# A hand-written order of attention and feed-forward steps, searched anew: which loads go first, and nine unread products inside one cluster

## The chip, the cores and the metric

One core of a Trainium2 chip runs the whole kernel. The core has five engines with queues of their own: TensorE (PE, matrix products into PSUM), VectorE (DVE), ScalarE (ACT), GpSimd (POOL) and SyncE (SP, which here only issues transfers). Each engine works through its queue in order and waits on semaphores. The metric is the time of one execution on the device in microseconds; lower is better.

## What is computed

Linear attention with a decay for each head, block by block, followed by a feed-forward layer with a leaky activation:

```python
for b in range(nb):                                   # blocks of 64
    intra = np.einsum('bhic,bhjc->bhij', qb, kb) * Dmask[None]
    intra = np.einsum('bhij,bhjd->bhid', intra, vb)
    inter = np.einsum('bhid,bhde->bhie', qb * lam_pow[None], kv_state)
    out[:, :, sl] = intra + inter
    kv_state = lam_block * kv_state + np.einsum('bhsd,bhse->bhde', kb * rev_pow, vb)
x = out.transpose(0, 2, 1, 3).reshape(B * S, H * D)
h = x @ w_in
g = np.maximum(h, 0.0) + alpha * np.minimum(h, 0.0)
y = g @ w_out
```

q, k and v are 4 x 8 x 768 x 64 (sequences, heads, positions, head width), w_in is 512 x 2048 and w_out 2048 x 512, all in fp32.

## The kernel before

The work is cut into six chunks of 512 tokens (`NC`), each of two sequences by 256 positions. A unit `n` is a chunk, one of its two sequences and one half of the heads, so units 0 to 3 are chunk 0, units 4 to 7 chunk 1, and so on up to 23.

For each unit `cast` writes q and k as halves (`qk16`), `turn` transposes them on PE and `turned` copies the result out of PSUM (later units are transposed by a load, `turn_by_dma`, on SP). `decayed` multiplies q by its decay (`qdT`) and `key_decayed` k by its own (`kdec`, four buffers). `decay_mask` and `causal` make the mask. `cluster(old, new)` is a run of small products on PE: for the older unit the state's part (L344) and the masked scores by v (L374), for the newer one the scores (L362) and then k by v (L391), which `state` and `spread` turn into the next state (`R`, `RD`). `masked` multiplies scores by the mask on DVE, and `out_of` copies the finished rows into `xT`.

The feed-forward part of a chunk `c` goes by sixteen blocks `f` of 128 columns: `up(c, f, bi, slot)` multiplies xT by w_in into a bank of PSUM (`bi` names one sequence, `None` both), `below` makes the lower branch on ACT, `gate` joins the branches on DVE (with `oma`, the slopes that `slopes` gets from alpha by a transposition on PE) and thereby frees the bank. `down` multiplies by w_out. From chunk 2 on the down product, and in chunk 5 also the up product, is done with seven products of sums of blocks in place of eight products (`product`, `up_block`, with `weight_sum`, `gate_sum`, `win_sum` and `x_sum`).

w_in is loaded in four pieces (`load_win(i)`, blocks 4i to 4i+3) and w_out likewise (`load_wout(i)`), all on POOL's queue and turned into halves on the way, as are v and the first q's (`load16`). k and the later q's are loaded in fp32 (`load`) on SP, or on POOL with `ring=1`. `hold` is a one-element memset on DVE ahead of a load, which keeps the load from being issued before DVE gets there. `fill(n, slot)` is `n` products of the identity with itself whose result nobody reads.

What runs when is written out by hand: a list of some 950 calls, one step a line, ends the kernel function. Each call appends its instructions to the queues of the engines that it names, so the list sets the order on every engine, and semaphores do the rest. PSUM has banks 0, 1 and 2 for `up` and `down`, `tk` for transposed tiles and the second half of products, two for scores and two for `acc`. A cluster called with `other=True` takes banks 0 and 1 in place of `acc`.

Of the kernel before, what the change touches and what calls it, by code (L numbers as in the profile page):

```python
# [11 lines left out]
def kernel(  # L12
# [315 lines left out]
    def cluster(old, new, other=False):  # L328
# [53 lines left out]
        if new is not None:  # L382
            t["kv"] = kv
            for hp in range(2):
# [62 lines left out]
    G = {}  # L447
# [343 lines left out]
    positions()  # L791
    load_alpha()
    identity()
    load("k", 0, 0, 0)
    distances()
    zeros(2, 1, "G")
    zeros(1, 1)
    logs()
    load16("q", 0, 0, 1)
    load("k", 0, 0, 1)  # L800
    fill(16, 2)
    key_decay(1)
    key_decay(0)
    load("q", 0, 0, 0)
    load16("v", 0, 0, 0)
    fill(36, 2)
    zeros(0, 1, "G")
    cast(0, "k", "V")
    hold("k", 1, 0)
    zeros(1, 0, "G")  # L810
    hold("k", 0, 1, 0)
    decay_mask(1, 1)
    key_decayed(1, "V")
    decay_mask(1, 0)
    cast(1, "k", "G")
    state_decay()
    decay_mask(0, 0)
    decay_mask(0, 1)
    cast(1, "q", "V")
    causal(0, 1)  # L820
    decay_mask(3, 0)
    cast(0, "q", "G")
    decay_mask(2, 0)
    load16("q", 0, 1)
    load("k", 0, 1, 1)
    turn(0)
    decay_mask(2, 1)
    query_decay(1)
    causal(1, 0)
    fill(5, 2)  # L830
    turned(0, "A")
    cast(3, "k", "A")
    zeros(0, 0)
    query_decay(0)
    key_decayed(0, "V")
    load16("v", 0, 0, 1)
    load16("v", 0, 1)
    load("k", 0, 1, 0)
    query_decay(3)
    fill(6, 2)  # L840
    turn(1)
    turned(1, "A")
    causal(0, 0)
    cluster(None, 0)
    fill(15, 2)
    key_decayed(3, "V")
    zeros(3, 1)
    key_decayed(2, "V")
    fill(17)
    spread(0, 1, "A", True)  # L850
    masked(0, 1)
    masked(0, 0)
    decay_mask(3, 1)
    load_win(0)
    cast(2, "k", "A")
    cast(2, "q", "V")
    cast(3, "q", "A")
    query_decay(2)
    state(0, 0)
    turn(2)  # L860
    causal(1, 1)
    load("k", 1, 0)
    decayed(0, "G")
    turned(2, "A")
    cast(5, "k", "V")
    slopes(2)
    load16("q", 1, 0)
    cluster(0, 1, True)
    state(0, 1)
    masked(1, 0)  # L870
    masked(1, 1)
    load16("v", 1, 0)
    decayed(1, "G")
    turn(3)
    spread(1, 1, "A", True)
    cluster(1, None)
    load_win(1)
    state(1, 0)
    hold("k", 3, 0)
    cast(4, "k", "A")  # L880
    out_of(0, "V")
    out_of(1, "A")
    load16("q", 1, 1)
    decayed(2, "V")
    state(1, 1)
    cluster(None, 2)
    masked(2, 1)
    hold("k", 2, 1)
    turned(3, "A")
    up(0, 0, 0, 2)  # L890
    spread(2, 1, "A", True)
    state(2, 0)
    load_win(2)
    masked(2, 0)
    key_decayed(4, "G")
    decayed(3, "G")
    below(0, 0, 0)
    gate(0, 0, 0)
    cast(4, "q", "G")
    cluster(2, 3, True)  # L900
    up(0, 2, 0, 2)
    load_win(3)
    spread(8, 0, "A")
    hold("k", 2, 0)
    cast(6, "q", "G")
    below(0, 2, 0)
    masked(3, 0)
    cast(7, "q", "G")
    spread(3, 1, "A", True)
    state(2, 1)  # L910
    state(3, 0)
    masked(3, 1)
    cast(5, "q", "V")
    state(3, 1)
    key_decayed(5, "G")
    zeros(2, 0, "G")
    turn(4)
    spread(11, 0, "V")
    out_of(2, "A")
    gate(0, 2, 0)  # L920
    cluster(3, None)
    fill(14, 0)
    load16("v", 1, 1)
    out_of(3, "A")
    turned(4, "V")
    load_wout(1)
    up(0, 1, 0, 0)
    below(0, 1, 0)
    up(0, 3, 0, 2)
    up(0, 6, None, 1)  # L930
    below(0, 3, 0)
    below(0, 6, None)
    gate(0, 1, 0)
    turn(5)
    cluster(None, 4)
    zeros(3, 0)
    state(4, 0)
    gate(0, 3, 0)
    gate(0, 6, None)
    turned(5, "A")  # L940
    decayed(5, "G")
    load_wout(0)
    hold("k", 1, 1)
    load("k", 1, 1)
    up(0, 2, 1, 0)
    below(0, 2, 1)
    decayed(4, "G")
    masked(4, 1)
    load_wout(2)
    up(0, 5, None, 2)  # L950
    up(0, 4, None, 1)
    state(4, 1)
    load("k", 2, 0, ring=1)
    gate(0, 2, 1)
    up(0, 0, 1, 0)
    below(0, 5, None)
    below(0, 4, None)
    gate(0, 5, None)
    below(0, 0, 1)
    up(0, 8, None, 2)  # L960
    gate(0, 0, 1)
    cast(6, "k", "G")
    below(0, 8, None)
    up(0, 3, 1, 0)
    spread(12, 0, "G")
    key_decayed(6, "G")
    gate(0, 4, None)
    gate(0, 8, None)
    below(0, 3, 1)
    up(0, 7, None, 1)  # L970
    masked(4, 0)
    spread(4, 1, "A")
    gate(0, 3, 1)
    load_wout(3)
    up(0, 1, 1, 2)
    cluster(4, 5)
    below(0, 7, None)
    cast(7, "k", "G")
    up(0, 9, None, 0)
    below(0, 1, 1)  # L980
    out_of(4, "A")
    state(5, 0)
    gate(0, 7, None)
    gate(0, 1, 1)
    up(0, 11, None, 2)
    below(0, 9, None)
    up(0, 14, None, 1)
    spread(5, 1, "A")
    below(0, 11, None)
    masked(5, 1)  # L990
    state(5, 1)
    gate(0, 9, None)
    below(0, 14, None)
    masked(5, 0)
    gate(0, 11, None)
    gate(0, 14, None)
    turn(6)
    key_decayed(7, "G")
    up(0, 12, None, 0)
    below(0, 12, None)  # L1000
    up(0, 10, None, 2)
    turned(6, "V")
    cluster(5, None)
# [767 lines left out]
```

## Time and profile before

| | |
|---|---|
| median of 3 runs | 209.84 us (209.22 to 210.29) |
| profiled execution, whole | 210.01 us |
| its span in the profile | 208.2 us |
| PE busy | 198.1 us |
| DVE busy | 173.2 us |
| ACT busy | 124.8 us |
| POOL busy | 124.5 us |
| bytes moved by transfers | 33.03 MB |
| unread products | 109, busy 9.8 us |

The profile is one execution. Its views are: a table of forty equal slices with the busy share of each engine in tenths, a list of who waited for whom, the chain of work that ended last, groups of like instructions with their mean time, the time from issue to landing of transfers, and a timeline in order of time. In a timeline row the first number is the start in microseconds from the start of the span, the second the length of the run of instructions, and `[2.72 <-POOL ident]` says how long the engine had been idle before it and what ended that. PE's matmuls overlap, so the sum of its busy time is no measure of how close it is to its peak; the distance between the starts of like products is.

### The profile page before, as it was taken

To read this page: it belongs to the slowest core of one execution; us is meant where nothing else is said; L and a number is where in the kernel's file an instruction comes from. 1 tells how busy PE (TensorE), PEld (TensorE's weight loads), DVE (VectorE), ACT (ScalarE), POOL (GpSimd) and SP (SyncE) were. 2 spreads that over 40 slices of the span, in tenths; PEclk is the share of its full clock that TensorE was granted. 3 is DMA by queue.
4 is the path that set the end of the run, shared out by engine and by line. 5 is a ranking of instruction groups with operands and counts; after the bars stand their busy time and mean duration, and the time that the engine had idled before them with its cause. 6 is when DMAs were issued, how large, how long until landed. Compare 5 with 4: busy or idle time off the path is not lost.

```text
span 208.2 us, 5964 instructions
## 1 busy us (share of the span) xinstructions
PE 198.1 (95%) x2382; PEld 134.7 (65%) x2382; DVE 173.2 (83%) x353; ACT 124.8 (60%) x257; POOL 124.5 (60%) x159
## 2 busy tenths in 40 slices
PE   4896899999999999999999999999999999999993
PEld 4874655565564564555556667776766688888882
DVE  3897889877587999788988899989978879998941
ACT  3997668753496644564777574646456567665320
POOL 8987289951293885787699542590389657235000
PEclk9999999999999999999999999999999999999999
DMA  4999999999999999999999899288160103102223
GB/s 114 272 188 191 200 216 167 199 285 204 137 302 244 240 278 202 291 261 157 202 230 172 108 194 186 74 213 97 23 131 2 55 0 105 50 0 78 76 76 126
DMA packets 61835, 33.03 MB, mean 159 GB/s; under 512 B 34528, under 2 KB 58608, under 8 KB 61808
## 3 DMA queue, kind: packets, MB, share of 16 engines
q0 software_dynamic: 22384, 13.24, 43.2%
q1 hardware_dynamic: 38096, 17.31, 37.5%
q10 hardware_dynamic: 1328, 2.11, 2.8%
q8 instruction: 18, 0.29, 0.6%
q14 instruction: 9, 0.07, 0.1%
HBM read 27.28 MB, written 6.29 MB: 161 GB/s over the span
## 4 chain that ended last, share of the span: by engine, by line
PE 76%; DMA 7%; issue 5%; POOL 4%; DVE 4%; ACT 1%; SPq 0%; POOLq 0%; DVEq 0%; ACTq 0%
PE h_ps L457 34%; PE p_ps L601 16%; PE o_ps L491 14%; DMA w_in_sb<-in_moe_w_in_dram 4%; PE s L362 3%; PE h_pb L705 3%; DMA qraw<-in_q_dram 3%; PE acc L374 2%; PE acc L344 2%; DVE g L752 2%; PE acc L391 1%; POOL win_sum L661 1%; POOL m L740 1%; DVE g L481 1%; POOL vh L102 1%
## 5 line engine op out<-in xcount | busy, mean ns | idle before, releaser
L457 PE MATMUL h_ps<-xT,w_in_sb 128*128 128x512 f16 (+1 forms) x352 | 77.3, 360 | 1.4 <-DMA w_in_sb<-in_moe_w_in_dram 0.9
L481 DVE SCALAR_TENSOR_TENSOR g<-m,oma,h_ps 128x512 f16<-128x512 f32 (+1 forms) x88 | 59.7, 694 | 15.7 <-ACT m L468 14.7
L468 ACT ACTIVATE m<-h_ps 128x512 f32<-128x512 f32 (+1 forms) x88 | 48.0, 558 | 34.3 <-PE h_ps L457 31.4
L457 PEld LDWEIGHTS <-w_in_sb 128*128 128x128 f16 x352 | 33.2, 98 | 30.9 <-issue 1.6
L601 PEld LDWEIGHTS <-g 128*128 128x128 f16 x320 | 31.1, 98 | 6.7 <-issue 0.2
L403 DVE TENSOR_TENSOR sm<-s,dmask 128x512 f16<-128x512 f32 x48 | 32.1, 683 | 1.4 <-PE s L362 1.4
L491 PE MATMUL o_ps<-w_out_sb,g 128*128 128x512 f16 x128 | 29.8, 379 | 0.0
L279 POOL TENSOR_TENSOR kdec<-kraw,kdecay 128x512 f16<-128x512 f32 x15 | 16.0, 1069 | 10.3 <-DMA kraw<-in_k_dram 6.9
L491 PEld LDWEIGHTS <-g 128*128 128x128 f16 x128 | 12.1, 98 | 13.5
L601 PE MATMUL p_ps<-wsum,g 128*128 128x256 f16 x160 | 20.6, 273 | 0.0
L601 PE MATMUL p_ps<-w_out_sb,g 128*128 128x256 f16 x160 | 19.9, 273 | 0.0
L252 POOL COPY RD<-R 64x128 f16<-64x128 f16 x30 | 9.1, 305 | 15.5 <-DVE R L428 14.6
L321 POOL TENSOR_TENSOR qdT<-qkT,qdecay 128x512 f16<-128x512 f16 (+1 forms) x15 | 15.9, 1064 | 3.1 <-DMA qkT<-qk 1.7
L248 ACT ACTIVATE xT<-acc 128x512 f16<-128x512 f32 x17 | 10.1, 596 | 8.0 <-PE acc L391 3.7
L625 ACT ACTIVATE o_sb<-p_ps 128x512 f32<-128x512 f32 (+1 forms) x20 | 10.2, 510 | 7.4 <-PE p_ps L601 7.1
L601 PEld LDWEIGHTS <-gsum 128*128 128x128 f16 x128 | 12.4, 98 | 2.7 <-DVE gsum L573 0.5
L428 DVE SCALAR_TENSOR_TENSOR R<-R,rdecay,acc 128x64 f16<-128x64 f16 x60 | 13.7, 273 | 0.6 <-ACT xT L248 0.3
L248 ACT ACTIVATE RD<-R 64x128 f16<-64x128 f16 x36 | 11.0, 306 | 2.8 <-DVE R L428 2.3
L238 PE MATMUL op_fill<-ident 128*128 128x128 f16 x109 | 9.8, 262 | 2.9 <-POOL ident masks.py:199 2.7
L601 PE MATMUL p_ps<-wsum,gsum 128*128 128x256 f16 x96 | 12.1, 273 | 0.2 <-DVE gsum L573 0.2
L581 POOL DMA_DIRECT2D g<-g x6 | 5.9, 978 | 10.7 <-PE p_ps L601 8.4
L102 POOL DMA_DIRECT2D vh<-in_v_dram x13 | 12.0, 926 | 0.0
(111 smaller groups left out, 315.4 us busy)
## 6 DMA issues: line engine op xcount, KB each, us to landing
out_dram<-o_sb SPq DMA_DIRECT2D x32, 128.0 KB, 2.0
kraw<-in_k_dram SPq DMA_DIRECT2D x7, 512.0 KB, 5.8
qraw<-in_q_dram SPq DMA_DIRECT2D x6, 512.0 KB, 6.9
vh<-in_v_dram POOLq DMA_DIRECT2D x11, 256.0 KB, 7.6
w_in_sb<-in_moe_w_in_dram POOLq DMA_DIRECT2D x4, 512.0 KB, 9.7
w_out_sb<-in_moe_w_out_dram POOLq DMA_DIRECT2D x4, 512.0 KB, 9.3
out_dram<-o_sb ACTq DMA_DIRECT2D x8, 256.0 KB, 5.5
kraw<-in_k_dram POOLq DMA_DIRECT2D x3, 512.0 KB, 10.2
```

Source lines behind the costliest of these rows:

```text
L102: nc.gpsimd.dma_start(out=rows16(x, c, bi)[:, ds(h0, n), :], in_=source({"q": q, "v": v}[x], c, bi, h0, n))
L248: nc.scalar.activation(out, in_, AF.Copy)
L279: engine(eng).tensor_tensor(out=kdec, in0=kr, in1=d.unsqueeze(3).to_broadcast([128, 2, 4, D]), op=ALU.mult)
L321: engine(eng).tensor_tensor(out=x, in0=y, in1=d.unsqueeze(2).to_broadcast([128, 4, n, 64]), op=ALU.mult)
L403: nc.vector.tensor_tensor(out=t["sm"][hl], in0=t["s"][hl], in1=mask_of(hl, units[n][2]), op=ALU.mult)
L428: nc.vector.scalar_tensor_tensor(out=then[:, hp], in0=R[b, hh, i][:, hp], scalar=rdecay[:, 2 * hh + hp : 2 * hh + hp + 1], in1=kv[:, hp], ...
L457: nc.tensor.matmul(h_ps[:, 0:n] if bi is None else h_ps[:, 0:n].rearrange("p (e j) -> p e j", e=2), lhsT=w_in_sb[:, gi, ts(f, 128)], rhs=x ...
L468: nc.scalar.activation(m[:, 0:n], HP[c, f, bi][:, 0:n], AF.Relu, scale=-1.0)
L481: nc.vector.scalar_tensor_tensor(out=g, in0=mv, scalar=oma[:, f : f + 1], in1=hv, op0=ALU.mult, op1=ALU.add)
L491: nc.tensor.matmul(O[c, t], lhsT=gated(c, f)[:, t // 2, t % 2, :], rhs=w_out_sb[:, f, :], start=(f == 0), stop=(f == NF - 1),)
L601: nc.tensor.matmul(acc, lhsT=lhsT, rhs=rhs, start=(first and j == 0), stop=(j == NJ - 1), skip_group_check=True,)
L625: nc.scalar.activation(o, acc, AF.Copy, scale=-1.0 if k in (7, 4) else 1.0)
```

## The change

`cluster` gets a parameter that puts unread products between its scores and its k by v, one call of it uses this, and the whole list of calls is replaced by another one. The steps are the same: the same products, the same loads, the same casts. What differs is their order and, for some hundred of them, the engine that does them.

```diff
-    def cluster(old, new, other=False):
+    def cluster(old, new, other=False, pad=0):
...
         if new is not None:
             t["kv"] = kv
+            if pad:
+                fill(pad, 2)
...
-    cluster(0, 1, True)
+    cluster(0, 1, True, 9)
...
-    load_win(1)
+    load("k", 1, 1, ring=1)
```

In the start, the new list has three memsets of `RD` on POOL ahead of the identity, 36 unread products, `slopes`, and 16 more ahead of `turn(0)` (before: 16, 36, `turn(0)`, and `slopes` behind `turn(2)`); the 32 products that stood behind `cluster(None, 0)` stand ahead of it, the 14 that stood behind `cluster(3, None)` stand ahead of `up(0, 0, 0)`. `load_win(1)` is ahead of `load16("v", 1, 0)` and `load_win(2)` ahead of `load16("q", 1, 1)`; `load_win(3)` is behind `key_decayed(5)`. `load_wout` goes in the order 0, 1, 2, 3 (before 1, 0, 2, 3), the last behind `weight_sum(1, 0, "G")`, which was on DVE. Four loads of k and q change between SP and POOL: `load("k", 1, 1)` goes to POOL, `load("k", 2, 1)`, `load("k", 3, 0)` and `load("q", 3, 0)` to SP. On DVE there are fewer `key_decayed` (6 for 9) and `decayed` (5 for 9), and more `out_of` (four more) and `win_sum` (11 for 7).

More of the change, by code (lines that the diff above doesn't have):

```diff
@@ L972 @@
[L972 to L995, printed above, removed]
@@ L996 @@
-    gate(0, 14, None)
-    turn(6)
-    key_decayed(7, "G")
[L999 to L1003, printed above, removed]
+    decayed(1, "G")
+    masked(1, 0)
+    state(1, 0)
+    state(1, 1)
+    cluster(1, None)
+    turned(2, "A")
+    key_decayed(2, "G")
+    out_of(1, "A")
+    cast(4, "k", "A")
+    turn(3)
+    out_of(0, "V")
+    cluster(None, 2)
+    turned(3, "V")
+    fill(14, 0)
+    up(0, 0, 0, 2)
+    masked(2, 0)
+    spread(2, 1, "A", True)
@@ L1115 @@
[L1115 to L1136 removed]
+    down(0, 3, 1, 2)
@@ L1247 @@
[L1247 to L1257 removed]
+    cluster(12, 13)
+    masked(13, 1)
+    cast(17, "q", "G")
+    up(2, 3, None, 0)
+    gate(2, 1, None)
+    weight_less(0)
+    below(2, 3, None)
+    out_of(12, "V")
+    down(1, 3, 0, 2)
+    gate(2, 3, None)
+    load("q", 4, 1)
+    weight_sum(3, 1, "G")
@@ L1565 @@
+    gate_sum(4, 4, 0, "k")
     up(4, 14, None, 0)
```

1416 lines of the change are left out of this document (709 added, 707 removed).

## The prediction

> **What bounds the kernel now.** I read the page's table of slices first, then the chain of waits, the waits of PE, and the timeline of the first 45 us.
>
> ```profile
> span 208.2 us, 5964 instructions
> PE 198.1 (95%) x2382; PEld 134.7 (65%) x2382; DVE 173.2 (83%) x353; ACT 124.8 (60%) x257; POOL 124.5 (60%) x159
> PE   4896899999999999999999999999999999999993
> PEclk9999999999999999999999999999999999999999
> PE op_fill L238 <- POOL ident masks.py:199: 2.7, 1, 2.7
> PE h_ps L457 <- DMA w_in_sb<-in_moe_w_in_dram: 0.9, 1, 0.9
> ```
>
> From the sixth slice (26 us) to the last, PE is full, and its longest waits are both in the start: 2.7 us before the first unread product and 0.9 us for the first piece of w_in. So a reordering can win only in the start, in small waits up to about 32 us, and in the tail, and can lose anywhere. The start on PE (start, length, what):
>
> ```profile
> 2.72 5.89 PE L238 MATMUL op_fill<-ident 128*128 128x128 f16 x52 [2.72 <-POOL ident masks.py:199]
> 8.45 0.61 PE L291 MATMUL tp<-ident,qk 128*128 128x128 f16 x8
> 11.39 2.18 PE L238 MATMUL op_fill<-ident 128*128 128x128 f16 x32
> 19.84 0.61 PE L457 MATMUL h_ps<-xT,w_in_sb 128*128 128x256 f16 x4 [0.92 <-DMA w_in_sb<-in_moe_w_in_dram]
> 23.52 0.95 PE L238 MATMUL op_fill<-ident 128*128 128x128 f16 x14
> 24.53 1.90 PE L457 MATMUL h_ps<-xT,w_in_sb 128*128 128x256 f16 x12
> 34.13 2.76 PE L457 MATMUL h_ps<-xT,w_in_sb 128*128 128x512 f16 x12
> ```
>
> Unread products fill the wait for data, 0.113 us each in the first 52 (5.89/52) and 0.068 later (2.18/32). Dense work begins at 24.53. In the row at 34.13 twelve products follow each other at 0.22 us, so `up(0, 14)`, the last third of them, begins at about 36.0. The end, from the chain:
>
> ```profile
> 195.68 0.70 DVE gsum L573
> 196.43 8.48 PE p_ps L601 x76
> 204.94 0.42 DVE o_sb L623
> ```
>
> PE finishes at 204.9 and 3.3 us of adding, storing and closing follow. Both lists end with the same products, the second half of `gate_sum(5, 2, 1)` before `product(5, 6, 0)` and one DVE add behind the last product; I cost the tail at nothing, and at 0.4 us (one DVE row more) if its two last adds queue.
>
> **The change, part by part.** Its products are those of before and nine unread ones; I cost it in four steps, made against the profiled execution (210.01 us, of which 208.2 are span).
>
> *1. The first unread products begin later, and DVE waits for them.* Three memsets of RD now stand on POOL ahead of `ident`.
>
> ```profile
> 2.85 0.51 POOL L175 MEMSET RD<- 128x512 f16 x1
> 6.11 0.43 DVE L250 CAST qk<-kraw 128x512 f16<-128x512 f32 x1
> 7.08 0.94 POOL L252 CAST qk<-qraw 128x512 f16<-128x512 f32 x1
> ```
>
> Three at 0.51 put PE's start at 2.72 + 1.5 = 4.2. Then come 36 unread products (36 x 0.113 = 4.1) and the transposition of alpha, so at 8.4 DVE can write `oma`, which now stands ahead of its first cast. The order of DVE, `oma` being the slopes and `qk` the halves of q and k, before:
>
> ```order
> L192 COPY llp<-loglam 64x4
> L250 CAST qk_246<-kraw 128x512
> L85 MEMSET kraw 1x1 x2
> L279 TENSOR_TENSOR kdec<-kraw,kdecay 128x512
> L250 COPY qk_257<-qh 128x512
> ```
>
> and with the change:
>
> ```order
> L192 COPY llp<-loglam 64x4
> L230 TENSOR_SCALAR oma<-at_ps 128x16
> L250 CAST qk_242<-kraw 128x512
> L85 MEMSET kraw 1x1 x2
> L279 TENSOR_TENSOR kdec<-kraw,kdecay 128x512
> ```
>
> So the cast moves from 6.11 to about 8.6, and all of DVE behind it, with the memsets that release two k loads on SP. `turn(0)` follows 16 more unread products at about 10.2 (8.45 before); POOL's cast of q (8.02) has long ended. Then 0.45 of turning and 32 x 0.068 = 2.2 put `cluster(None, 0)` at 12.9, where the rows of before have it at 10.91.
>
> ```profile
> 10.91 0.42 PE L362 MATMUL s<-qkT 64*64 64x128 f16 x16
> 12.77 1.28 DVE L403 TENSOR_TENSOR sm<-s,dmask 128x512 f16<-128x512 f32 x2
> 14.16 0.55 DVE L207 TENSOR_TENSOR dmask<-dmask,keep 128x384 f32<-128x384 f32 x1
> 16.77 0.76 DVE L250 CAST xT<-h_acc 128x256 f16<-128x256 f32 x2
> 22.89 0.28 DVE L250 COPY qk<-qh 128x512 f16<-128x512 f16 x1
> 23.23 0.47 DVE L428 SCALAR_TENSOR_TENSOR R<-R,rdecay,h_acc 128x64 f16<-128x64 f16 x2
> 24.16 0.48 DVE L481 SCALAR_TENSOR_TENSOR g<-m,oma,h_ps 128x256 f16<-128x256 f32 x1
> 24.56 0.68 DVE L250 COPY qkT<-tp 128x1024 f16<-128x1024 f16 x1
> ```
>
> The scores are ready at about 13.3. From the first `masked` to `masked(3, 1)` DVE has 8 masks (0.64), 2 causal masks (0.5), 3 casts from halves (0.28), a `decayed` (0.4), 4 pairs of states (0.46), the 2 halves of `out_of(0)` (0.76), `turned(3)` (0.65) and a gate (0.45): 11.1 us. So `cluster(3, None)` can end at 13.3 + 11.1 + 0.4 = 24.8. Before it ended at 23.52, but 14 unread products stood behind it until 24.53; these now stand ahead of `up(0, 0, 0)`, where PE waits for `out_of(0)` and the weights, and `up(0, 1, 0)` (0.44) is done before the cluster. On equal work: 24.8 - 0.44 - 24.53 = -0.2 us. This is the term that I trust least: without POOL's memsets or at 0.068 a product it falls by 1 us or more, with DVE a tenth slower it grows by 1.1.
>
> [...]
>
> *2. The nine unread products* stand between the two halves of `cluster(0, 1)`: 9 x 0.068 = 0.6 us of PE. PE reaches `turn(2)` at 17.1 with them, while `cluster(1, None)` waits for DVE's `masked(1, 0)` until 18.3. Hidden; 0.6 us if DVE is early.
>
> *3. Loads.* POOL's queue of loads before, from the first piece of w_in:
>
> ```order
> L110 DMA w_in_sb<-in_moe_w_in_dram 128x4x512
> L321 TENSOR_TENSOR qdT<-qkT,qdecay 128x4x64
> L102 DMA qh<-in_q_dram 128x8x128
> L102 DMA vh<-in_v_dram 128x8x128
> L321 TENSOR_TENSOR qdT<-qkT,qdecay 128x4x64
> L110 DMA w_in_sb<-in_moe_w_in_dram 128x4x512
> L102 DMA qh<-in_q_dram 128x8x128
> L110 DMA w_in_sb<-in_moe_w_in_dram 128x4x512
> ```
>
> and with the change:
>
> ```order
> L110 DMA w_in_sb<-in_moe_w_in_dram 128x4x512
> L102 DMA qh<-in_q_dram 128x8x128
> L110 DMA w_in_sb<-in_moe_w_in_dram 128x4x512
> L102 DMA vh<-in_v_dram 128x8x128
> L321 TENSOR_TENSOR qdT<-qkT,qdecay 128x4x64
> L279 TENSOR_TENSOR kdec<-kraw,kdecay 128x512
> L110 DMA w_in_sb<-in_moe_w_in_dram 128x4x512
> ```
>
> The second piece passes the values of chunk 1, and the third passes their second q. Landings, by tile:
>
> ```profile
> L110 POOL DMA_DIRECT2D w_in_sb<-in_moe_w_in_dram x1: 759/759/759, 17.2 to 17.2; - x1
> DMA to landing us min/median/max: 12.0/12.0/12.0
> L110 POOL DMA_DIRECT2D w_in_sb<-in_moe_w_in_dram x1: 792/792/792, 21.9 to 21.9; - x1
> DMA to landing us min/median/max: 9.8/9.8/9.8
> ```
>
> Pieces three and four landed at 29.2 and 31.7, so a piece takes 2.5 us of a full queue, and the q or v of a sequence about 1.5 (half the bytes). Issue times of the first piece slip 0.9 us (POOL casts q and k one after the other ahead of the loads); the queue in front of it is as long as before, so it lands at about 20.4 instead of 19.8, when `up(0, 0, 0)` is ready anyway (20.5). Counting on from there: second piece 24.4 (used at 25.4), values of chunk 1 25.9 (used at 27.1), third piece 28.4 (used at 28.9). The fourth is issued behind `kdec` of units 4 and 5 at about 26.2 and lands at 34.2 (used at 35.8). POOL's load of k for units 6 and 7 (on SP before) waits for a memset that DVE reaches at 21.9; behind it stand `decayed(3)` (ready 23.5, used at 23.8) and `kdec(4)` (24.5, used at 27.1). Three later loads of k and q go the other way, to SP, behind its transposing loads; where POOL waits for such a k now, PE does not notice:
>
> ```profile
> 51.32 1.05 POOL L279 TENSOR_TENSOR kdec<-kraw,kdecay 128x512 f16<-128x512 f32 x1 [4.83 <-DMA kraw<-in_k_dram]
> ```
>
> Step 3 costs nothing, but its covers are 0.5 to 1.6 us wide; a queue 10% slower costs about 1.
>
> *4. From `cluster(3, None)` to `up(0, 14)`.* The work there is 10.1 us (six halves of `up` less one at 0.44, seven whole at 0.865, a turn 0.45, clusters 1.4). I lay it out by banks: `up(0, 6)` waits 0.25 for `out_of(3)`, `up(0, 7)` 0.45 for `gate(0, 4)`, `up(0, 9)` 0.25 for `gate(0, 3)`. 24.8 + 10.1 + 0.95 = 35.85 against 36.0. Beyond it PE is full in both; DVE, the next in load, gets lighter:
>
> ```profile
> L279 DVE TENSOR_TENSOR kdec<-kraw,kdecay 128x512 f16<-128x512 f32 x9 | 7.7, 861 | 0.6 <-PE acc L391 0.5
> L321 DVE TENSOR_TENSOR qdT<-qkT,qdecay 128x512 f16<-128x512 f16 x7 | 6.1, 875 | 0.8 <-DMA qkT<-qk 0.8
> ```
>
> Three `kdec` and five such `qdT` fewer are 7.0 us, of which other steps take about 4 back; hidden under PE, and nothing either way.
>
> Sum: -0.2 us at `up(0, 14)`, nothing behind it: 209.8 for the profiled execution, which is 0.17 above the median of the runs shown, so **209.6 us**: no change.
>
> **Rivals.** *Faster start.* The fills are quicker or DVE has less to wait for than I reckon, and the start is bound by w_in alone: `up(0, 0, 0)` at 20.4, then only its gate (0.44 + 0.6 + 0.5) before `up(0, 2, 0)`, and `cluster(3, None)` ends at about 23.8: 1.0 less, 208.6, and with the three waits of step 4 halved 208.2. For it: before paid 0.95 us of unread products at 23.52 with its weights landed. Against it: DVE's late cast.
>
> *DVE late (the other side).* POOL's memsets and casts slow DVE: `llp` beside two of them took 1.02 where its twin took 0.20, and a `kdec` 0.90 where another took 0.62.
>
> ```profile
> 4.84 0.20 DVE L191 COPY llp<-loglam 64x4 f32<-64x4 f32 x1 [0.28 <-ACT loglam L189]
> 5.06 1.02 DVE L192 COPY llp<-loglam 64x4 f32<-64x4 f32 x1
> 5.03 1.02 POOL L175 MEMSET RD<- 128x512 f16 x2
> ```
>
> If the stretch from 8.6 to 24.8 is a tenth longer, every mask is late by up to 1.6 us: 211.2. It decides once DVE has no gap there, and I find only short ones.
>
> *Last piece of w_out late.* It is now issued behind `weight_sum(1, 0)` on POOL, which waits for the second piece (landing about 42) and takes 2.13 us:
>
> ```profile
> L545 POOL TENSOR_TENSOR wsum<-w_out_sb 128x1024 f16<-128x1024 f16 x2 | 4.3, 2132 | 0.0
> L89 POOL DMA_DIRECT2D kraw<-in_k_dram x1: 882/882/882, 41.0 to 41.0; - x1
> DMA to landing us min/median/max: 10.2/10.2/10.2
> ```
>
> Issue at 44.2 with two k and q loads ahead, landing at about 50.4, wanted by `down(0, 2, 3)` at 52. With the 10.2 us that this load of k took it lands at 54.4: PE stops 2.4 us, 212.0.
>
> *Clock.* If PE's waits of up to 1 us between 14 and 20 bring back the slow rate of the first products, some 3 us of `up` take 1.7 times as long (0.113/0.068): 211.5. In before PEclk is 9 throughout and waits of 0.9 us changed nothing. [...]
>
> **How the numbers follow.** No change 0.37, faster start 0.34, DVE late 0.14, w_out late 0.11, clock 0.04. What a measurement of this kernel tells from no change is about 0.5%, 1.05 us. So faster 0.34, same 0.37, slower 0.29. The likeliest case alone spans 208.9 to 210.7; the range takes in the faster start and most of the dear cases: 207.9 to 211.8.
>
> **What would show it.** Step 1: PE's first product at 4.2, `oma` at 8.4, the first cast on DVE at 8.6, `cluster(None, 0)` at 12.9, `cluster(3, None)` ending at 24.8. Step 2: a wait of PE for DVE between `turn(2)` and `cluster(1, None)`. Step 3: no wait for w_in or w_out over 0.3 us. Step 4: `up(0, 14)` at 35.9 and PE full from there to about 204.7. An end of `cluster(3, None)` before 24 or behind 25.8, or a stop of PE behind 36, would make it wrong.

## The result, and the profile after

| comparison on one chip | changed kernel | kernel before | ratio (95% interval) |
|---|---|---|---|
| first | 210.99 us (210.39 to 212.91, 17 executions) | 209.61 us (209.22 to 210.93, 17) | 1.0064 (1.0044 to 1.0085) |
| again, in later rounds (`new_again`) | 210.81 us (210.60 to 212.00, 12) | 209.98 us (209.13 to 213.37, 29) | 1.0043 (1.0017 to 1.0069) |

The change makes the kernel slower by 0.64%, 1.3 us, where no change was forecast (209.6 us). Ratios leave out executions that are more than 1.5% longer than the fastest of the same kernel, so the median of an experiment can stand far above its ratio.

The profiled execution of the changed kernel took 210.69 us. Its page, and PE's waits (in all, times, longest, in us):

```profile
span 208.6 us, 5977 instructions
...
PE 197.1 (94%) x2391; PEld 134.2 (64%) x2391; DVE 171.5 (82%) x349; ACT 125.5 (60%) x256; POOL 121.8 (58%) x162
...
PE   1978899999999999999999999999999999999992
```

```profile
PE op_fill L238 <- POOL ident masks.py:199: 4.2, 1, 4.2
PE h_acc L344 <- ACT qk L248: 1.3, 1, 1.3
PE acc L374 <- DVE sm L405: 0.6, 1, 0.6
```

From the sixth slice on PE stands at 9 but for one slice, nearly as before. No wait for w_in or w_out is left, and the 0.92 us for the first piece of w_in is gone. The waits in the start are now for ACT and DVE. PE's first 26 us:

```profile
4.20 3.87 PE L238 MATMUL op_fill<-ident 128*128 128x128 f16 x36 [4.20 <-POOL ident masks.py:199]
...
12.08 0.42 PE L362 MATMUL s<-qkT 64*64 64x128 f16 x16
...
15.32 0.27 PE L344 MATMUL h_acc<-qdT,RD 128*128 128x128 f16 x2 [1.32 <-ACT qk L248]
...
16.10 0.68 PE L238 MATMUL op_fill<-ident 128*128 128x128 f16 x9
...
18.65 0.42 PE L374 MATMUL acc<-sm,vh 64*64 64x128 f16 x16 [0.62 <-DVE sm L405]
...
20.89 0.61 PE L459 MATMUL h_ps<-xT,w_in_sb 128*128 128x256 f16 x4
...
25.39 1.83 PE L459 MATMUL h_ps<-xT,w_in_sb 128*128 128x256 f16 x9
```

The start is what the prediction laid out: the first unread product at 4.20 (4.2 forecast), `cluster(None, 0)` at 12.08 (12.9), the wait for DVE's masks before `cluster(1, None)` (0.62 until 18.65), `up(0, 0, 0)` at 20.89. But `cluster(3, None)` ends, and dense products begin, at 25.39 instead of 24.8.

The span falls into three parts: up to the dense products, from there to VectorE's last add, and the closing behind it. The new list has `up(0, 1, 0)` (0.44 us) done ahead of the first mark, so 0.44 is taken off there. Two profiles of each kernel, in us:

| profile | dense from | on equal work | last add begins | between | span | closing |
|---|---|---|---|---|---|---|
| before, first | 24.53 | 24.53 | 204.94 | 180.41 | 208.23 | 3.29 |
| before, second | 24.17 | 24.17 | 204.65 | 180.48 | 207.93 | 3.28 |
| changed, first | 25.39 | 24.95 | 204.99 | 180.04 | 208.64 | 3.65 |
| changed, second | 26.30 | 25.86 | 205.91 | 180.05 | 209.58 | 3.67 |

Three things are read from it. The long middle got 0.4 us shorter. The closing got 0.4 longer. And the start ends 0.4 to 1.7 later, where 0.2 sooner was forecast. The first profile of the changed kernel fell on the shortest span of its 17 executions (208.6; their median is 209.1, that of the kernel before 207.9 over 35 executions in later rounds). So the two first profiles, 0.4 us of span apart, show only a third of the loss.

The closing differs behind the last store. The last store's issue, and SyncE's waits for stores at the program's end (in all, times, longest, in us), first of the kernel before and then of the changed one:

```profile
205.39 0.33 SPq L628 DMA_DIRECT2D out_dram<-o_sb  x1
```

```profile
SPq L1766 <- DMA out_dram<-o_sb: 1.1, 2, 0.8
```

```profile
205.44 0.33 SPq L630 DMA_DIRECT2D out_dram<-o_sb  x1
```

```profile
SPq L1768 <- DMA out_dram<-o_sb: 1.4, 1, 1.4
```

Both stores land 1.8 us after their issue, at 207.24 and 207.29, and no engine computes behind them. At the program's end SyncE waits for eighteen semaphores, those of its transfers among them, in nine instructions that name two each and follow each other at 0.061 us where they need not wait. In the kernel before, the last store's semaphore stands in the eighth of them: seven are done while the store is under way, and one is left behind its landing. In the changed kernel it stands in the second, and seven are left. Six more at 0.061 are 0.37 us, which is what the closing grew by (3.28 and 3.29 to 3.65 and 3.67). The other traces agree. With the old list's start and end the closing is 3.27 to 3.29, with one wait behind the last store; the experiments below on the new list have 3.64 to 3.67, with seven in each trace that records the store's landing. Two of the splices lie between, with two waits (3.42) and six (3.59), and the third has seven (3.65). So the order of the transfers, which settles the semaphore of the last store, makes this part of the loss. No run was made that changes that semaphore alone.

### The profile page after: what moved, and what is told of

Read it like the earlier page. It is cut to its first block, busy times and chain, and to the rows that moved or that the text cites. A ratio compares the mean times of both kernels' runs of the same rounds, so it can differ in the third digit from the quotient of the medians.

```text
span 208.6 us, 5977 instructions
## 1 busy us (share of the span) xinstructions
PE 197.1 (94%) x2391; PEld 134.2 (64%) x2391; DVE 171.5 (82%) x349; ACT 125.5 (60%) x256; POOL 121.8 (58%) x162
## 4 chain that ended last, share of the span: by engine, by line
PE 82%; DVE 6%; issue 5%; POOL 4%; ACT 1%; POOLq 0%; DVEq 0%; ACTq 0%
PE h_ps L459 34%; PE p_ps L603 17%; PE o_ps L493 13%; PE op_fill L238 4%; PE s L362 4%; PE h_pb L707 3%; PE acc L374 3%; PE acc L344 2%; PE acc L393 1%; DVE g L754 1%; PE tp L291 1%; POOL win_sum L663 1%; POOL m L742 1%; DVE sm L405 1%; POOL RD L175 1%
## 5 line engine op out<-in xcount | busy, mean ns | idle before, releaser
L470 ACT ACTIVATE m<-h_ps 128x512 f32<-128x512 f32 (+1 forms) x88 | 48.5, 558 | 36.4 <-PE h_ps L459 34.7
L252 POOL COPY RD<-R 64x128 f16<-64x128 f16 x36 | 12.1, 335 | 25.1 <-DVE R L430 23.1
L321 POOL TENSOR_TENSOR qdT<-qkT,qdecay 128x512 f16<-128x512 f16 (+1 forms) x19 | 20.4, 1077 | 3.6 <-ACT qkT L248 3.0
L279 POOL TENSOR_TENSOR kdec<-kraw,kdecay 128x512 f16<-128x512 f32 x18 | 19.2, 1067 | 3.9 <-DMA kraw<-in_k_dram 3.5
L627 ACT ACTIVATE o_sb<-p_ps 128x512 f32<-128x512 f32 (+1 forms) x20 | 10.2, 510 | 9.7 <-PE p_ps L603 9.7
L102 POOL DMA_DIRECT2D vh<-in_v_dram x13 | 12.5, 966 | 0.2 <-issue 0.2
L238 PEld LDWEIGHTS <-ident 128*128 128x128 f16 x118 | 8.5, 113 | 5.0 <-POOL ident masks.py:199 4.2
L513 ACT ACTIVATE o_sb<-o_ps 128x512 f32<-128x512 f32 x8 | 4.8, 598 | 9.9 <-PE o_ps L493 9.8
```

The costliest lines, as they stand in the source:

```text
L102: nc.gpsimd.dma_start(out=rows16(x, c, bi)[:, ds(h0, n), :], in_=source({"q": q, "v": v}[x], c, bi, h0, n))
L238: nc.tensor.matmul(t[:, 0:128], lhsT=ident, rhs=ident, start=True, stop=True)
L252: nc.gpsimd.tensor_copy(out=out, in_=in_)
L279: engine(eng).tensor_tensor(out=kdec, in0=kr, in1=d.unsqueeze(3).to_broadcast([128, 2, 4, D]), op=ALU.mult)
L321: engine(eng).tensor_tensor(out=x, in0=y, in1=d.unsqueeze(2).to_broadcast([128, 4, n, 64]), op=ALU.mult)
L470: nc.scalar.activation(m[:, 0:n], HP[c, f, bi][:, 0:n], AF.Relu, scale=-1.0)
```

## The experiments

Eighteen kernels ran, each beside the kernel before on the same chip. All compute the whole result. Where an edit speaks of the list, it is the list of calls at the kernel's end.

| kernel | median (lowest to highest), executions | ratio to before (95%) |
|---|---|---|
| `s_new_start` | 214.25 (212.98 to 214.75), 6 | 1.0182 (1.0134 to 1.0230) |
| `s_old_start` | 214.87 (212.06 to 219.67), 6 | 1.0130 (1.0054 to 1.0207) |
| `s_new_17` | 213.29 (212.84 to 216.93), 6 | 1.0143 (1.0092 to 1.0194) |
| `nopad` | 213.07 (210.01 to 220.87), 12 | 1.0008 (0.9968 to 1.0049) |
| `new_again` | 210.81 (210.60 to 212.00), 12 | 1.0043 (1.0017 to 1.0069) |
| `old_again` | 209.94 (209.09 to 212.55), 12 | 0.9984 (0.9952 to 1.0016) |
| `slopes_late` | 215.42 (212.07 to 221.24), 6 | 1.0120 (1.0061 to 1.0179) |
| `old_slopes` | 215.28 (211.25 to 222.70), 12 | 1.0094 (1.0049 to 1.0139) |
| `holds_early` | 211.18 (210.70 to 212.41), 12 | 1.0070 (1.0042 to 1.0099) |
| `pool_start` | 211.11 (210.44 to 212.37), 12 | 1.0056 (1.0028 to 1.0084) |
| `q_on_act` | 210.75 (210.19 to 216.01), 12 | 1.0036 (1.0001 to 1.0070) |
| `nopad_c4` | 215.88 (214.42 to 218.56), 6 | 1.0239 (1.0182 to 1.0296) |
| `on_dve` | 211.36 (210.52 to 215.61), 12 | 1.0059 (1.0027 to 1.0090) |
| `on_dve_holds` | 211.08 (210.65 to 215.47), 12 | 1.0063 (1.0036 to 1.0090) |
| `pad18` | 211.09 (210.85 to 211.83), 12 | 1.0052 (1.0022 to 1.0082) |
| `old_win` | 210.72 (209.26 to 212.21), 12 | 1.0032 (0.9995 to 1.0068) |
| `added_early` | 211.33 (210.97 to 211.58), 5 | 1.0076 (1.0058 to 1.0094) |
| `all_three` | 210.98 (210.55 to 211.89), 6 | 1.0072 (1.0050 to 1.0094) |

### Splices of the two lists

```diff
 s_new_start: the new list up to down(0, 2, 0, 1), then the steps of the old list that are not done yet
 s_old_start: the old list up to down(0, 2, 0, 1), then the steps of the new list that are not done yet
 s_new_17:    the new list up to cluster(17, 18), then the steps of the old list that are not done yet
```

> The new list up to down(0, 2, 0) (about 43 us), then the old list for all that is left. Theory 'start' (the 1.3 us of the changed kernel are lost in the start, through slopes ahead of DVE's first cast, and vary from run to run with the first loads): about 1.2 to 1.4 us slower than before, like the whole change. Theory 'later' (the start is even, as the two profiles show with down(0, 2, 0) at 43.1 and 43.3; the loss comes behind it, in waits for loads that vary from run to run): within 0.3 us of before.

> The old list up to down(0, 2, 0), then the new list for all that is left. Theory 'start': within 0.3 us of before. Theory 'later': 1.0 to 1.4 us slower than before.

> The new list up to cluster(17, 18) (about 119 us), then the old list. Theory 'start': 1.2 to 1.4 us slower, as with the new start alone. Theory 'later' does not say by itself in which half; if the loss lies between 43 and 119 us, where the transfers are busy, this is 1.0 to 1.4 us slower, and if behind 119 us, within 0.3 us of before.

All three are 2 to 5 us above both lists by their medians. Each joint brought a wait that neither list has: 0.95 for a state at 52.15 and 0.78 for a gate at 45.42 (`s_new_start`), 2.83 for a transposing load at 61.10 (`s_old_start`), 1.8 for a weight sum (`s_new_17`). So they say nothing on where the loss lies: two orders that are each laid out to their end can't be cut in the middle.

### The nine unread products

```diff
 nopad
-    cluster(0, 1, True, 9)
+    cluster(0, 1, True)
 pad18
-    cluster(0, 1, True, 9)
+    cluster(0, 1, True, 18)
 nopad_c4: as nopad, and
-    cast(4, "q", "V")
+    cast(4, "q", "A")
```

> The changed kernel without the nine unread products in cluster(0, 1). Theory 'pad on the path': 0.5 to 0.6 us faster than the changed kernel, so 0.7 us slower than before. Theory 'hidden' (the prediction's step 2): as the changed kernel, 1.3 us slower than before. A third, that the nine keep the clock up: slower than the changed kernel, with small products at twice their distance behind 16 us.

> The changed kernel with eighteen unread products in the cluster instead of nine, 0.6 us more of PE. If they lie on the path: 0.4 to 0.7 us above the changed kernel, and the nine cost about as much. If PE only waits for VectorE behind them, as the prediction had it: within 0.2 us, with the wait of 0.62 for sm gone.

> The changed kernel without the nine unread products, and with the copy of q for unit 4 on ScalarE instead of VectorE. Without the nine alone, half of the runs took 215 to 221 us. Theory of the holds: there VectorE's copy stood still for 2.5 us or more behind four operations of POOL in a row, PE waited for it and its granted clock fell to one half; on ScalarE it can't, so all runs end at 209.6 to 210.6. Theory that the gap where the nine products stood brings the slow clock by itself: half of the runs stay at 215 or more.

Without the nine, six executions took 210.0 to 211.1 us, with a granted clock of 0.992 to 1.000 on the mean, and six 215.1 to 220.9 with 0.972 to 0.983. The profile is one of the latter (span 215.0). PE's busy time and granted clock in stretches of 2 us (stretch, length, busy, clock, then transfers):

```profile
16.00:18.00 2.00, 1.43 (x57) 1.00 1.47 201
18.00:20.00 2.00, 1.10 (x26) 1.00 1.42 197
20.00:22.00 2.00, 2.00 (x49) 0.60 1.49 198
...
26.00:28.00 2.00, 0.61 (x4) 0.80 1.43 195
28.00:30.00 2.00, 1.77 (x23) 0.50 1.38 300
```

At 16 to 20 the clock is full, and PE is busy for 2.5 of 4 us, behind a wait of 1.32 and with waits of 0.46 and 0.83. In the next two rows the clock is about one half. A second such stretch follows a wait of 1.91 us at 25.5. At half clock fourteen unread products take 1.68 us (0.95 in the changed kernel) and four products of `up` 1.06 (0.60), and what waits for them is late as well. So the nine products are no mere filling: with them the clock stayed up (1.00 in all stretches of the changed kernel's two profiles, and no execution of 29 above 212.91 us). The share of busy time in these 4 us does not decide it alone, for in the kernel before PE is busy for only 2.08 of the same 4 us, and the clock stays at 1.00; the last section has more on this. What the nine cost is read from the six executions without them that kept their clock: their lowest time is 0.4 us under the changed kernel's (210.01, 210.39), and their median, 210.28, is 0.5 to 0.7 under its medians. Their ratio to the kernel before, 1.0008 (0.9968 to 1.0049), does not tell the two apart. `pad18` puts its lowest time 0.25 to 0.46 above the two lowest of the changed kernel (210.39, 210.60), and its median 0.1 to 0.3 above the medians. The forecast had the nine hidden; by `nopad` 0.4 to 0.7 us lie on the path, most or all of their 0.6.

`nopad_c4` failed as a cure: its copy stood on ACT and not on VectorE, and yet all six executions took 214.4 us or more, with a mean clock of 0.974 to 0.992. In its profile the clock falls at 17.2, before that copy's place. So the late copy is not needed for the fall; the gap where the nine stood is enough, with the earlier waits as they were.

### What sets the start

```diff
 slopes_late
     fill(36, 2)
-    slopes(2)
...
     turn(2)
+    slopes(2)
 old_slopes (the old list)
+    zeros(1, 0, "G"); zeros(2, 1, "G"); zeros(0, 1, "G")      ahead of identity()
-    fill(16, 2)
+    fill(36, 2)
+    slopes(2)
...
-    fill(36, 2)
+    fill(16, 2)
 holds_early
+    hold("k", 2, 0); hold("k", 0, 1, 0)                       ahead of slopes(2)
 pool_start
-    zeros(1, 0, "G"); zeros(2, 1, "G"); zeros(0, 1, "G")      ahead of identity()
+    the same behind load16("q", 0, 0, 1)
 q_on_act
-    cast(3, "q", "V"); cast(2, "q", "V")
+    cast(3, "q", "A"); cast(2, "q", "A")
```

> The changed kernel once more, for a second profile beside the kernel before in the same rounds. By the theory that the new start is bound by VectorE's own chain and the old one by w_in's first landing: the products after the start are dense again from about 25.4 us on, within 0.3 of the first profile (25.39), and the time stands 1.0 to 1.5 us above the kernel before. By the rival that late transfers cost it, a wait that ends in a transfer or in a cast behind one appears in this profile which the first did not have, or the start shifts by over 0.5 us.

> The kernel before once more, for a second profile of it. By the theory that the first profile of it fell on a late landing of w_in (0.92 us of wait there), this one has that wait shorter by 0.5 us or more, a span of 207.2 to 207.8 and its last product at 204.0 to 204.5 instead of 204.94. By the rival that the loss lies after the last product, the last product ends at 204.9 again, and the part of the span behind it is 3.0 us or less, against 3.6 in the changed kernel.

> The changed kernel with slopes(2) moved behind turn(2), so that VectorE's first cast no longer stands behind the 36 cold fills and oma. By the theory that VectorE's start binds the new list: first cast at about 6.1 to 6.6 us instead of 8.6, cluster(None,0) 1 us or more earlier, and the time 0.8 to 1.5 us under the changed kernel, 209.3 to 210.2. By the rival that the nine products or later waits carry the loss, the time stays within 0.3 us of the changed kernel. By the rival of the granted clock, the earlier start only lengthens a wait between 14 and 28 us, slices of that stretch show a granted clock of 0.5 to 0.8, and the time is 212 or more.

> The kernel before with the new list's start: three memsets on POOL ahead of the identity, 36 fills and slopes ahead of VectorE's first cast. By the theory that VectorE's start binds: first cast at about 8.6 us instead of 6.1, and the time 0.8 to 1.5 us above the kernel before. By the theory that w_in's first landing binds the old start whatever VectorE does, within 0.3 us of it.

> The changed kernel with the two one-element memsets that release SP's loads of k moved ahead of slopes, so that they are done at about 6.1 us instead of 9.3. Theory of the queue: the idle stretch of the DMA engines at 8 to 11 us disappears, w_in's first piece lands at 19.2 to 19.8 instead of 20.9, up(0,0,0) begins up to 1 us earlier and the time falls by 0.4 to 1.0 us against the changed kernel. Theory of the chain over VectorE: w_in lands earlier just the same, but up(0,0,0) still begins at 20.7 to 22 and the time stays within 0.3 us of the changed kernel.

> The changed kernel with the identity and the first two half loads ahead of the three memsets on POOL. Theory of the late start: PE's first product at 2.7 instead of 4.2, lamc free of POOL's DMA issue (0.17 instead of 0.91), ScalarE's exponentials 0.7 earlier, oma at about 6.9, cluster(None,0) at 11.0 to 11.4 instead of 12.1, and the time 0.6 to 1.1 us under the changed kernel. Theory of the holds (VectorE's copies from halves stand still while POOL computes): the start moves earlier, but the copies at 13 to 16 us take 0.8 us or more each in the same way, and no more than 0.4 us is left of it. By the queue theory w_in's first landing caps the gain at 0.4 too, with a wait of PE for w_in in the profile.

> The changed kernel with the copies of q for units 2 and 3 on ScalarE instead of VectorE. Theory of the holds: the two took 1.13 and 0.30 us on VectorE in the first profile (0.60 and 0.28 in the second, behind a qdT of 1.98) against 0.28 each when POOL computes nothing, so VectorE reaches masked(1,1) 0.9 to 1.4 earlier, PE's wait of 0.62 for it goes, and the time falls by 0.4 to 0.9 us. Theory of the late start or of the queue: up(0,0,0) still begins at 20.8 or later, and the time stays within 0.3 us of the changed kernel.

`new_again` and `old_again` are the table above. The start shifts by 0.9 us from one execution of the changed kernel to the next, and the whole rest goes with it. `old_again` fits neither of its expectations: its last add came at 204.65, 0.29 sooner, and the closing stayed at 3.28 against 3.67. So the loss lies in the start and in the closing both.

`slopes_late` refutes my first theory, that VectorE's first cast sets the start. The cast ran at 6.11, and VectorE then waited for a table of decays from ScalarE until 8.62, and for a mask of ScalarE until 9.95, when the same operation begins in the changed kernel:

```profile
8.62 0.69 DVE L279 TENSOR_TENSOR kdec<-kraw,kdecay 128x512 f16<-128x512 f32 x1 [1.71 <-ACT kdecay L212]
9.95 0.56 DVE L207 TENSOR_TENSOR dmask<-dmask,keep 128x384 f32<-128x384 f32 x1 [0.64 <-ACT dmask L202]
```

ScalarE makes its exponentials in another order now (two for q and two masks among those for k), and its logarithm ahead of them begins 0.70 later (5.30 for 4.60). It waits for VectorE's `lamc`, which took 0.91 us in the first profile and ended with an issue of POOL (5.27 and 5.30). That the issue held it is not shown: in the kernel before, `lamc` took 0.17 beside an issue too. `old_slopes` costs the old list 2.1 us in its best execution (211.25 to 209.13): its dense products begin at 26.05, and the clock in its profile fell to 0.58 at 18 to 22 us. So that start costs, but the run can't part the late chain from the clock.

`holds_early` brings w_in's first piece 1.7 us sooner, 8.5 us after its issue at 10.7 instead of 10.2:

```profile
L110 POOL DMA_DIRECT2D w_in_sb<-in_moe_w_in_dram x1: 792/792/792, 10.7 to 10.7; - x1
...
DMA to landing us min/median/max: 8.5/8.5/8.5
```

`up(0, 0, 0)` still began at 20.87 and the time stayed. So w_in alone does not bound the new start. `pool_start` had PE begin at 2.72, and `cluster(None, 0)` at 11.46. Then VectorE waited 1.24 us for a q that the earlier k's had pushed back (8.1 us from issue to landing, 4.4 in the changed kernel):

```profile
16.42 0.52 DVE L250 COPY qk<-qh 128x512 f16<-128x512 f16 x1 [1.24 <-DMA qh<-in_q_dram]
```

`q_on_act` took the copies off VectorE. The next operation in line then took 1.40 us instead of 0.55, and PE's waits changed places. Each edit moved one bound, and the next stood in its place some tenths behind.

### VectorE beside POOL

Between 14 and 17 us VectorE's operations are long in the changed kernel. VectorE, then POOL, in its first profile:

```profile
14.41 0.86 DVE L321 TENSOR_TENSOR qdT<-qkT,qdecay 128x256 f16<-128x256 f16 x1
15.20 1.13 DVE L250 COPY qk<-qh 128x512 f16<-128x512 f16 x1
...
16.72 0.30 DVE L250 COPY qk<-qh 128x512 f16<-128x512 f16 x1
```

```profile
14.32 0.67 POOL L321 TENSOR_TENSOR qdT<-qkT,qdecay 128x256 f16<-128x256 f16 x1 [0.32 <-ACT qkT L248]
14.95 1.23 POOL L279 TENSOR_TENSOR kdec<-kraw,kdecay 128x512 f16<-128x512 f32 x1
```

The copy of 128x512 halves takes 0.30 at 16.72, where POOL issues a load, and 1.13 at 15.20, where it computes; it ends 0.15 behind POOL's `kdec`. `qdT` takes 0.86 (0.41 in the profile before) and ends at 15.27, 0.28 behind POOL's `qdT` and while POOL's `kdec` is running. PE's wait of 1.32 us, which the page puts down to ScalarE, ended 0.05 behind it. In the second profile POOL came first, and `qdT` took 1.98, through both operations, to 0.29 behind the end of the second:

```profile
14.66 1.98 DVE L321 TENSOR_TENSOR qdT<-qkT,qdecay 128x256 f16<-128x256 f16 x1
16.57 0.60 DVE L250 COPY qk<-qh 128x512 f16<-128x512 f16 x1
```

```profile
14.61 0.74 POOL L321 TENSOR_TENSOR qdT<-qkT,qdecay 128x256 f16<-128x256 f16 x1
15.25 1.10 POOL L279 TENSOR_TENSOR kdec<-kraw,kdecay 128x512 f16<-128x512 f32 x1
```

```profile
16.70 0.27 PE L344 MATMUL h_acc<-qdT,RD 128*128 128x128 f16 x2 [2.44 <-DVE qdT L321]
...
26.30 0.97 PE L459 MATMUL h_ps<-xT,w_in_sb 128*128 128x256 f16 x5
```

PE waited 2.44 us for it, and dense products begin 0.9 later than in the first profile. In these rows what VectorE runs beside POOL's two operations ends 0.15 to 0.29 us behind the end of one of them: `qdT` behind the first in the first profile (15.27 to 14.99) and behind the second in the second (16.64 to 16.35). Why it is once the one and once the other is not shown.

`on_dve` and `on_dve_holds` give POOL's two operations to VectorE:

```diff
     decayed(0, "V")
+    decayed(1, "V")
...
-    decayed(1, "G")
...
-    key_decayed(2, "G")
...
+    key_decayed(2, "V")
     out_of(0, "V")
 on_dve_holds: the same, and holds_early
```

> The changed kernel with POOL's qdT of unit 1 and kdec of unit 2 (14.3 to 16.2 us) on VectorE instead: 0.3 and 0.65 us more for VectorE, and POOL computes nothing while VectorE makes its own qdT and the copies of q. Theory of the holds: VectorE's qdT falls from 0.86 to about 0.3, the copies from 1.13 to about 0.3, VectorE ends masked(3,1) 0.4 to 1.0 sooner in spite of the added work, and the time falls by 0.3 to 0.9 us against the changed kernel. Theory of mere load on VectorE: its durations stay, the added 0.95 lies on its chain, and the time grows by 0.5 to 1.0 us.

> The same with the two memsets that release SP's loads of k ahead of slopes as well, so that w_in's first piece lands at about 19.2 instead of 20.9. If both bounds of up(0,0,0) are then moved (theory of holds and queue together): up(0,0,0) before 20.4, dense products from 24.8 or sooner and 0.3 us or more below on_dve. If w_in's landing is no bound in the new list: the same as on_dve within 0.3 us.

```profile
14.30 0.75 DVE L321 TENSOR_TENSOR qdT<-qkT,qdecay 128x256 f16<-128x256 f16 x2
14.97 0.29 DVE L250 COPY qk<-qh 128x512 f16<-128x512 f16 x1
...
22.44 3.56 DVE L250 COPY qk<-qh 128x512 f16<-128x512 f16 x1
```

Two `qdT` take 0.75 together and the copies 0.29 and 0.28: with a second `qdT` to do by then, VectorE began the masks of unit 1 at 16.23, 1.09 sooner than in the first profile, and PE's wait for `qdT` was 0.87 instead of 1.32. So the holds, operations of VectorE made long by POOL's beside them, are real, and mere load is refuted. The next bound stood close behind: `up(0, 0, 0)` now waited 0.57 us for w_in and began at 20.96, no sooner than before. In this execution another copy met an issue and four operations of POOL in a row (22.60 to 25.84) and took 3.56; PE waited 2.67 and the clock fell (0.75 on the mean from 26 to 30 us). In `on_dve_holds`, with w_in earlier too, `up(0, 0, 0)` began at 20.12; the copy came earlier and took 0.28, and dense products began at 24.39, 1.0 sooner than in the first profile of the changed kernel:

```profile
24.39 2.48 PE L459 MATMUL h_ps<-xT,w_in_sb 128*128 128x256 f16 x12
```

And yet its time is that of the changed kernel. The lead is lost later, in two places.

### Where an earlier start goes

PE waits at 119.70 for a gate of VectorE, which waits for a transfer that adds into `gsum`:

```profile
119.70 1.67 PE L459 MATMUL h_ps<-xT,w_in_sb 128*128 128x512 f16 x7 [1.24 <-DVE g L483]
```

```profile
118.29 0.69 DVE L575 TENSOR_TENSOR g<-g,gsum 128x1024 f16<-128x1024 f16 x1 [1.63 <-DMA gsum<-g]
```

```profile
L583 POOL DMA_DIRECT2D gsum<-g x1: 1209/1209/1209, 107.2 to 107.2; - x1
...
DMA to landing us min/median/max: 11.0/11.0/11.0
```

The changed kernel's first profile has the same transfer issued at 107.02, landing after 9.6, with 0.9 us to spare. `q_on_act` (0.69) and `pad18` (0.93) show this wait as well: it comes and goes with the landing, 8.0 to 11.7 us in the runs with the new list where the transfer was not moved.

```diff
 added_early
+    gate_added(2, 1, 0)
     load16("v", 5, 0)
...
-    gate_added(2, 1, 0)
 all_three: on_dve_holds and added_early
```

> The changed kernel with the accumulating transfer into gsum of chunk 2 (gate_added(2,1,0)) issued ahead of a load of values and a kdec on POOL, 2 us or more sooner. Its first profile had no wait there, a margin of 0.9 us. Theory that the start alone makes the loss: time within 0.2 us of the changed kernel, the best runs at 210.4 to 210.6. Theory that the late landing also lengthens other runs: the median falls by 0.2 to 0.5 us, the best runs stay. In both, no wait of PE for VectorE's g at 119 us.

> POOL's two operations on VectorE, SP's loads of k released early, and gate_added(2,1,0) issued early. If the start and this transfer are the two bounds of the new list: dense products from about 24.4, no wait at 119, a span of 207.6 to 208.2, time 209.2 to 209.9, 1.0 us or more under the changed kernel and about that of the kernel before. If another bound stands behind: 210.5 or more, with a wait of PE over 0.5 us somewhere behind 30 us that shows it.

Issued early, the transfer stopped nobody. The changed kernel's time stayed (211.33 over five executions, best 210.97), so in it this transfer is not the loss. `all_three` kept its lead of 0.7 us over the changed kernel up to 155 us (24.71 for 25.39 at the dense products, 155.24 for 155.93 at the last scores) and had lost it at 174. There PE stops three times for 0.2 to 0.3 us:

```profile
170.11 0.60 PE L707 MATMUL h_pb<-x_sum,w_in_sb 128*128 128x256 f16 x4
170.78 0.60 PE L707 MATMUL h_pb<-xT,win_sum 128*128 128x256 f16 x4
...
172.30 0.61 PE L707 MATMUL h_pb<-x_sum,win_sum 128*128 128x256 f16 x4
```

Its chain of waits (start, length, what) goes mostly over VectorE from 164.83 to 173.44:

```profile
164.83 0.76 DVE g L483
...
167.83 0.98 DVE gsum L575
...
172.16 0.68 DVE o_sb L625
172.84 0.60 DVE h_sum L726
...
173.49 0.60 PE h_pb L707 x4
```

VectorE's busy time in one stretch of the last chunk (stretch, length, busy), of the kernel before, the changed one and `all_three`:

```profile
170.00:175.00 5.00, 4.29 (x8) 1.00 0.32 107
```

```profile
170.00:175.00 5.00, 5.00 (x11) 1.00 0.32 108
```

```profile
170.00:175.00 5.00, 5.00 (x10) 1.00 0.24 82
```

Over 155 to 175 VectorE has 17.17 us of 20 before, 19.27 in the changed kernel and 19.72 in `all_three`. The new list moved sums of gates and of w_in from POOL to VectorE there: POOL makes one sum of gates between 152 and 190 us (2.45 us) where it made three (2.16 each). So in that execution VectorE bounds the stretch, and the lead had nowhere to go.

### The old list with w_in first

```diff
 old_win (the old list)
+    load_win(0)
     load16("v", 0, 1)
...
-    load_win(0)
```

> The kernel before with w_in's first piece issued ahead of the values of the second sequence, so that it lands at about 18.5 instead of 19.8. Theory that w_in's first landing makes the old list's spread: PE's wait of 0.92 for w_in goes, the time falls by 0.4 to 0.8 us in the median and the best runs stay at about 209.0. Theory that VectorE and PE bind the old start as well: up(0,0,0) still begins at 19.4 or later and the time stays within 0.2 us; by the clock rival or a late landing of the values (wanted at 18.6) it is 0.5 us or more slower.

```profile
19.04 0.32 PE L391 MATMUL acc<-vh,kdec 64*64 64x64 f16 x16 [1.14 <-DMA vh<-in_v_dram]
...
24.22 1.90 PE L457 MATMUL h_ps<-xT,w_in_sb 128*128 128x256 f16 x12
```

The wait for w_in went, and one of 1.14 us for the values took its place; dense products began at 24.22, as in `old_again`. So what makes the old list's best executions (spans from 207.2 us) shorter than its two profiles is left open. No kernel beat the kernel before.

## Why the prediction was wrong

**Step 1, the start, is the step that failed.** It forecast `cluster(3, None)` at 24.8 and -0.2 us on equal work; measured were 25.39 and 26.30 in the two profiles, +0.4 and +1.3 against the first profile of the kernel before. Its head was right: 4.20, 8.42 and 8.62 for forecast 4.2, 8.4 and 8.6 (the 36 products took 3.87 us where the row gave 4.1), and the scores were even ready 0.76 early (first mask at 12.54 for 13.3), as the 16 products behind `oma` ran at 0.066 each (1.05/16) where 0.113 was reckoned. What failed is the 11.1 us of VectorE from the first mask to the last. I took the copies at 0.28 and `qdT` at 0.4 from rows that POOL did not lengthen, and the new order puts POOL's `qdT` and `kdec` beside them. The masks took 12.24 us in the first profile (12.54 to 24.78), and 12.9 in the second. In the first, `qdT` took 0.86 and two of the three copies 1.13 and 0.83 (the last beside an issue of POOL, 22.23 to 23.12, though other copies beside an issue took 0.3), 1.9 more than reckoned. The rest of the stretch took 0.7 less than the sum had it, since a row's length runs up to 0.1 into the next row. So 0.76 early, 1.14 more and a last step of 0.6 for 0.4 give 25.39 for 24.8. The mechanism stood among the rivals as "DVE late", at 1.6 us and a chance of 0.14; so its chance was too small, and its place was not the whole stretch but three operations.

My own reading of that loss was wrong at first too: neither the first cast, nor the k's released late, nor w_in's landing sets the start by itself. And no edit to the start shortened the whole time, so that VectorE's holds make the start late is shown, and that they cost the whole program as much is not.

**Step 2** forecast nine hidden products. PE did wait for VectorE behind them, as forecast, but 0.4 to 0.7 us show in the executions without them that kept their clock, and what they do is to keep the clock up: at 21 to 23 us it is 1.00 in the changed kernel's two profiles and 0.50 in that of `nopad`.

**Step 3** held: no load stopped PE in the first profile. The first piece of w_in landed at 20.9 (20.4 forecast). The transfer at risk was one that the step did not name, the sum into `gsum` at 107 us.

**Step 4** forecast a middle of equal length and "nothing either way" from a lighter VectorE. The middle is 0.4 us shorter, a gain that was missed and whose cause was not sought. VectorE is lighter over the span (171.5 for 173.2) but fuller in the last chunk (19.27 of 20 us for 17.17), which `all_three` shows to bind as soon as PE comes earlier. And the tail, costed at nothing, is the second term that failed: the products and the last adds are the same, but seven of SyncE's waits in place of one stand behind the last store, 0.37 us more.

**The rivals.** The late piece of w_out did not come. The clock, at 0.04, did not fall in the changed kernel, so it was rightly left out of the sum. Its reason, that waits of 0.9 us changed nothing in the kernel before, did not carry: without the nine products the clock did fall, behind waits of 1.32 us and less, and in `nopad` PE was busy for 2.05 of the 3.41 us ahead of the fall. The faster start was wrong about w_in alone: with w_in landed at 19.2, `up(0, 0, 0)` still began at 20.87.

Sum on the medians: 209.1 - 207.9 = 1.2 us of span in the first comparison, 209.0 - 208.2 = 0.8 in the second. The closing gives 0.4 and the middle takes 0.4, so 0.8 to 1.2 is the start. The nine products are 0.4 to 0.7 of that, and the rest is VectorE and ScalarE later, by the holds beside POOL and the later exponentials, whose shares vary from one execution to the next and were not parted.

## What to carry to other kernels

Price an operation by rows in which the other engines do what they will do beside it: here a copy cost 0.28 or 3.56 us, by what POOL did at the time. Before giving an engine more work because its share of the whole span is low, look at its share in the stretch where the work goes. And when one edit to a start changes nothing, ask which bound stands some tenths behind: here VectorE, ScalarE and the loads stood in a row, and a start 0.7 us earlier was used up 150 us later. And look at what follows the last store: here the place of one semaphore among the final waits cost 0.37 us.

## What was not expected of the hardware

In `nopad` TensorE's granted clock is full up to 20.38 us, one half to 23.79, full to 27.21 and one half to 34.03. These stretches last 3.41 us or a multiple of it, and so do those of `slopes_late` (half clock from 19.72 to 23.13) and `nopad_c4` (17.24 to 24.08). In the 3.41 us ahead of a fall PE was busy for 2.05 and 1.59 us in `nopad` and 1.89 in `slopes_late`. Of the windows of that length, counted from the first full clock on, that full clock followed, one in `new_again` held 1.80 us of PE's work (with a single wait of 2.44 us), one in the first profile of the kernel before 1.91 (202.99 to 206.40), one in `old_again` 1.98, and in the first profile of the changed kernel none held less than 2.54 (14.62 to 18.03). So between 1.8 and 2.05 us of work it went both ways, and a wait of 2.44 us went without a fall where waits of 1.32, 0.46 and 0.83 in `nopad` came ahead of one; what decides, these runs do not show. VectorE's copy from halves took 2.81 us in `nopad`, 3.47 in `slopes_late` and 3.56 in `on_dve`, there beside four of POOL's operations (22.60 to 25.84), against 0.28 at 22.89 in the profile before, where POOL ran nothing; an operation with two float32 inputs (`dmask`, 0.55) took 1.40 in `q_on_act`, where POOL's `kdec` ran from 15.15 to 16.38.
